# DeltaNet followed by soft-MoE slots: a planned instruction order, an inverse built from halves, and outputs re-laid on chip

## The chip, the cores and the metric

The kernel runs on one core of a Trainium2 chip. The metric is the device time of one execution in microseconds (us). Everything is fp32. The core has five instruction queues that run side by side and each take their instructions strictly in order: TensorE (PE, matrix products into PSUM), VectorE (DVE), ScalarE (ACT), GpSimd (POOL), and SyncE (SP), which here only issues DMAs. An instruction that waits holds up everything behind it on its own queue.

## The reference

Two blocks follow each other. The first is a delta-rule attention over 768 time steps for 4 batches and 8 heads of width 48; its output is laid out as 3072 tokens of 384 numbers. The second is a soft mixture of 8 experts with 4 slots each.

```python
k_n = k / (norm(k) + 1e-6)
for t in range(S):                              # S = 768, per batch and head, D = 48
    y[t] = q[t] @ state
    state += beta[t] * outer(k_n[t], v[t] - k_n[t] @ state)
x = y as (3072 tokens, 384)
logits = x @ phi                                # phi: 384 x 32 slots
d = softmax(logits, over tokens);  slot_in = d.T @ x          # 32 x 384
slot_out[e] = relu(slot_in[e] @ w1[e]) @ w2[e]  # w1: 384 x 1024, w2: 1024 x 384, 8 experts
out = softmax(logits, over slots) @ slot_out    # 3072 x 384
```

## The kernel before

**The scan.** Time is cut into 24 chunks of 32 steps; four chunks make a group, of which there are six. The 32 heads of all batches are handled together: the 128 partitions are four heads of a half-set times 32 steps, and the free dimension runs over 4 batches and 2 half-sets. Within a chunk the recurrence becomes matrix products. With T the inverse of a unit lower triangular 32x32 matrix made of beta and K K', a chunk computes the residual R = V - K S (`psR`, L278, then DVE at L283), solves U = T R (`psW`, L289, copied by ACT at L292), updates the state S += K' U (`psS`, L299, copied by ACT at L311 and DVE at L309 into the other of two block-diagonal state tiles), and gives Y = Q S + A U (`psY`, L278 and L316, copied at L318). Only R, U and S depend on the chunk before; everything else is preparation.

**Preparation** of a chunk (`prep`): K and Q arrive by DMA as 32-partition pieces (four DMAs of 48 KB for each tensor and chunk, L80), are padded from 48 to 64 columns, transposed on PE (L173) and copied by ACT (L176). Then Gram products of K with K and Q (L188) give the triangular matrix `Lc` and the masked `AT` (L195).

**Inversion** of a group (`invert`): DVE transposes `Lc` so that each partition holds one whole 32x32 matrix (128 matrices at once), the norms of k are formed by DVE and an ACT square root (L221 to L233), POOL scales the matrix (L230), and then 31 elimination steps run on DVE. Step j multiplies one row by one column into `pr` (L240) and subtracts that from all rows below (L243), so there are 62 operations, each of which needs the one before. POOL scales the result (L247), DVE transposes it back (L253).

**Routing** of a group (`route`): the outputs are transposed on PE with 96 columns at a time (L336), multiplied by phi (L345), and go through both softmaxes; the token softmax keeps a running maximum. `repeat` spreads the weights with products against the identity (L398), `slots` adds the weighted outputs in 64 small products (L410).

**Order.** A loop over chunks issues all of this. `chunk` calls `fill()` between its products; each call issues a quarter of a list in which the preparation of the chunk eight ahead, a quarter of the next group's inversion and a quarter of the last group's routing are interleaved evenly. Weights of two experts are loaded during the scan; all others get buffers only when the scan's pools are closed (`att.close()`). They arrive as whole 1.5 MB DMAs on SP.

**The tail**: two passes of four experts each (`first`: L543, relu, transposes L556; `second`: L567), a fold over experts, then 24 output tiles of 128 tokens (L593), copied by DVE and ACT in turn and stored through six buffers `ob` on SP.

## Time and profile before

| what | us |
|---|---|
| median of 3 runs (lowest, highest) | 493.28 (489.14, 493.31) |
| span of the profiled execution | 489.7 |
| elimination on DVE, L240 and L243, 186 instructions each, busy | 68.0 and 66.3 |
| residual L283, 24 instructions, mean of one | 0.55 |
| state copies, ACT L311 and DVE L309, mean of one | 0.80 and 0.96 |
| POOL products L230 and L247, six each, mean of one | 1.91 and 1.91 |
| weight loads w1 and w2, 8 each of 1.5 MB, median to landing | 8.2 and 15.1 |
| loads of K, Q, V, 96 of each, 48 KB, median to landing | 2.3 |

One execution was recorded by the hardware profiler. "Busy" is the time in which an engine had at least one instruction running. PEld is the loading of the stationary operand, which runs beside PE. The granted clock (PEclk) is a share of TensorE's full clock. A group is all instructions of one source line. An idle stretch of an engine is put down to whatever released it last. The chain is the work that ended last, followed backwards.

### The profile page before, as it was taken

How to read it: one execution, taken by the hardware profiler on the slowest of the kernel's cores; microseconds unless marked ns; L12 is line 12 of the kernel's file. 1: busy time of each engine (PE TensorE's matmuls, PEld its weight loads, DVE VectorE, ACT ScalarE, POOL GpSimd, SP SyncE). 2: the span in 40 equal slices, each digit the busy share in tenths (PEclk: the TensorE clock that was granted, in tenths of full speed). 3: DMA queues.
4: the chain of work that ended last, by engine and by line, in shares of the span. 5: the costliest groups of instructions: out<-in, count | busy, mean ns of one | idle time of the engine just before them, and what ended most of it. 6: DMA issues, size and time to landing. Idle time of an engine off the chain costs nothing.

```text
span 489.7 us, 20564 instructions
## 1 busy us (share of the span) xinstructions
PE 334.7 (68%) x9387; PEld 248.3 (51%) x9387; DVE 245.1 (50%) x679; ACT 128.9 (26%) x257; POOL 63.6 (13%) x88
## 2 busy tenths in 40 slices
PE   5743374656766758788677776876875865788586
PEld 4532263545645646666466655665664753532133
DVE  4159716972168942379721788325997212210033
ACT  2331122121322422332422233224312222111012
POOL 9210112012020040020210200202301000000000
PEclk9655556665766759755778577599798797799695
DMA  6557742320322213202221110010300029949427
GB/s 114 86 94 195 205 83 51 52 37 18 52 51 39 46 19 52 50 16 40 51 39 33 19 19 13 9 20 5 113 23 1 4 94 367 424 156 434 208 101 287
DMA packets 84759, 45.53 MB, mean 93 GB/s; under 512 B 79392, under 2 KB 82624, under 8 KB 82624
## 3 DMA queue, kind: packets, MB, share of 16 engines
q1 hardware_dynamic: 81920, 43.67, 32.4%
q8 instruction: 74, 1.21, 1.0%
q10 hardware_dynamic: 2176, 0.39, 0.4%
q0 software_dynamic: 576, 0.15, 0.3%
q14 instruction: 13, 0.11, 0.1%
HBM read 39.47 MB, written 4.72 MB: 90 GB/s over the span
## 4 chain that ended last, share of the span: by engine, by line
DVE 27%; issue 25%; PE 19%; SPq 10%; DMA 10%; POOL 5%; ACT 3%; DVEq 0%; POOLq 0%; ACTq 0%
DVE pr L240 9%; SPq L80 9%; DVE tt L243 9%; DMA w2t<-in_moe_w_dram 4%; PE pso L567 3%; DVE S L309 3%; PE psR L278 2%; PE pt L410 2%; DMA w1t<-in_moe_w_dram 2%; PE psY L278 2%; POOL lb L230 2%; DMA Q<-in_q_dram 2%; DVE TT L253 2%; PE ph L543 1%; DMA out_dram<-ob 1%
## 5 line engine op out<-in xcount | busy, mean ns | idle before, releaser
L240 DVE TENSOR_TENSOR pr<-tt,lb 128x31 f32<-128x31 f32 (+15 forms) x186 | 68.0, 365 | 17.7 <-POOL lb L230 12.2
L243 DVE TENSOR_TENSOR tt<-tt,pr 128x31 f32<-128x31 f32 (+15 forms) x186 | 66.3, 357 | 5.7
L289 PE MATMUL psW<-R,TT 32*32 32x48 f32 x1536 | 29.9, 242 | 47.0 <-DVE R L283 45.5
L173 PE MATMUL pt<-ident,K 128*128 128x128 f32 x96 | 36.0, 396 | 24.1 <-DVE AT L195 18.7
L289 PEld LDWEIGHTS psW<-R,TT 32*32 32x32 f32 x1536 | 25.7, 134 | 52.4 <-DVE R L283 49.3
L176 ACT ACTIVATE KQ<-pt 128x512 f32<-128x512 f32 x48 | 27.1, 595 | 73.9 <-PE pt L173 73.5
L278 PE MATMUL psR<-S,KQ 128*32 128x96 f32 x768 | 33.1, 324 | 17.7 <-DVE S L309 17.0
L316 PE MATMUL psY<-U,AT 32*32 32x48 f32 x1536 | 39.0, 256 | 3.2 <-issue 3.1
L195 DVE TENSOR_TENSOR AT<-pt,tri 128x128 f32<-128x128 f32 x48 | 11.9, 288 | 54.6 <-ACT Lc L194 54.4
L188 PE MATMUL pt<-KQ 48*32 48x64 f32 x1536 | 33.5, 246 | 6.2 <-ACT KQ L176 2.6
L309 DVE COPY S<-psS 48x768 f32<-48x768 f32 x23 | 22.1, 961 | 31.1 <-ACT S L311 30.7
L316 PEld LDWEIGHTS psY<-U,AT 32*32 32x32 f32 x1536 | 31.1, 143 | 9.2 <-issue 7.1
L299 PE MATMUL psS<-U,K 32*48 32x48 f32 x1472 | 25.3, 261 | 14.5 <-ACT U L292 11.6
L278 PEld LDWEIGHTS psR<-S,KQ 128*32 128x32 f32 x768 | 23.7, 145 | 22.4 <-DVE S L309 18.9
L188 PEld LDWEIGHTS pt<-KQ 48*32 48x32 f32 x1536 | 25.0, 119 | 16.0 <-ACT KQ L176 9.5
L173 PEld LDWEIGHTS pt<-ident,K 128*128 128x128 f32 x96 | 17.3, 186 | 30.7 <-DVE AT L195 20.2
L278 PE MATMUL psY<-S,KQ 128*32 128x96 f32 x768 | 32.3, 314 | 0.0
L292 ACT ACTIVATE U<-psW 128x384 f32<-128x384 f32 x24 | 11.8, 490 | 75.6 <-PE psW L289 75.6
L299 PEld LDWEIGHTS psS<-U,K 32*48 32x48 f32 x1472 | 20.4, 155 | 20.7 <-ACT U L292 15.7
L410 PE MATMUL pt<-Y,dr 32*32 32x97 f32 x768 | 25.1, 271 | 8.5 <-DVE AT L195 4.3
L230 POOL TENSOR_TENSOR lb<-lb,gm 128x1024 f32<-128x1024 f32 x6 | 11.5, 1911 | 141.0 <-DVE gm L229 141.0
L173 PE MATMUL pt<-ident,Q 128*128 128x128 f32 x96 | 29.7, 364 | 0.0
(124 smaller groups left out, 454.9 us busy)
## 6 DMA issues: line engine op xcount, KB each, us to landing
w1t<-in_moe_w_dram SPq DMA_DIRECT2D x8, 1536.0 KB, 8.2
w2t<-in_moe_w_dram SPq DMA_DIRECT2D x8, 1536.0 KB, 15.1
K<-in_k_dram SPq DMA_DIRECT2D x96, 48.0 KB, 2.3
V<-in_v_dram SPq DMA_DIRECT2D x96, 48.0 KB, 2.3
out_dram<-ob SPq DMA_DIRECT2D x24, 192.0 KB, 2.3
Q<-in_q_dram SPq DMA_DIRECT2D x88, 48.0 KB, 2.3
Q<-in_q_dram ACTq DMA_DIRECT2D x8, 48.0 KB, 3.0
bb<-in_beta_dram POOLq DMA_DIRECT2D x16, 6.0 KB, 3.0
```

Of the source, the lines that this page charges most:

```text
L80: eng.dma_start(out=dst[C * h:C * h + C, :, 0:D], in_=src.rearrange("b (g h) s d -> h s (b g) d", h=4)[h, cc * C:(cc + 1) * C])
L173: nc.tensor.transpose(tp[:, i, a, :], src[:, b * G:(b + 1) * G, :].rearrange("p g d -> p (g d)"), ident)
L176: nc.scalar.activation(KQ[cc][:, 2 * bh:2 * bh + 2], tp, ACT.Copy)
L188: nc.tensor.matmul(pg[g][rh, b], lhsT=KQ[cc][r, b, 0, rh], rhs=KQ[cc][r, b, :, rh], start=True, stop=True, skip_group_check=True)
L240: nc.vector.tensor_tensor(prv, tt[:, j, 0:m].unsqueeze(1).broadcast_to([P, w, m]), lb[:, j, j + 1:C].unsqueeze(2).broadcast_to([P, w, m]), ...
L243: nc.vector.tensor_tensor(tt[:, j + 1:C, 0:m], tt[:, j + 1:C, 0:m], prv, op=ALU.subtract)
L278: nc.tensor.matmul(dst[hs[h], b].rearrange("p g d -> p (g d)"), lhsT=kq[:, b, a, hs[h]], rhs=old[:, h, b, :], start=(b == 0), stop=False, ...
L289: nc.tensor.matmul(pw[hs[h], u], lhsT=T[hs[h], u], rhs=R[hs[h], u], start=(u == 0), stop=True, skip_group_check=True)
L299: nc.tensor.matmul(psS[DP * g:DP * g + D, h, b * D:(b + 1) * D], lhsT=K[hs[h], b * G + g, 0:D], rhs=Ut[hs[h], b * G + g], start=(cc == 0 a ...
L309: nc.vector.tensor_copy(dst, src)
L316: nc.tensor.matmul(py[hs[h], b, g], lhsT=at[hs[h], g, b], rhs=Ut[hs[h], b * G + g], start=False, stop=True, skip_group_check=True)
L410: nc.tensor.matmul(pa[r], lhsT=st["dr"][r, c, b, :], rhs=Yn[r, c, b, 0:GD + 1], start=(b == 0), stop=(b == B - 1), skip_group_check=True)
```

## The change

It is a rewrite of the whole kernel that computes the same thing.

*Order.* The kernel text no longer issues instructions; it records operations with the values they read and write, an engine (or a choice of two) and an assumed cost. `Plan.run` then places them: it repeatedly takes, for each engine, the operation of highest priority among those that can start within 0.15 us of the earliest one, and assigns buffers and PSUM banks as it goes. The priority is the longest path to the end by the assumed costs. The result is one fixed order for each queue. Evictions from PSUM, re-lay DMAs and stores get their engine from the plan.

*Memory.* All scan buffers lie in one arena, cut into pieces of the size of one expert weight (12 KB per partition). A first planning run tells in which order buffers die; they are packed into pieces in that order, and each piece becomes a weight buffer when all its members are dead. Weights are loaded in thirds (w1) and quarters (w2).

*Inverse.* The two diagonal 16x16 halves of the triangular matrix are inverted side by side in one set of 15 steps, 30 DVE operations; the lower left block is made on PE from two products of small tiles. The norms use two powers on POOL.

*Scan.* The state is no longer block-diagonal: reads of it become 32 products with 48 rows instead of 16 with 128. Half of the state accumulates in PSUM and is copied by ACT, the other half is added by DVE. K and Q lose their padding; their transposes are products with the identity as moving operand, 48 columns each.

*Routing.* Four DMAs per chunk move the output from its scan layout into rows of 32 tokens by 384, on chip. Transposes, logits and slot sums then run on whole 128-row tiles. beta arrives in one DMA and is spread by four products.

```diff
+    def run(self, backing=()):
...
+                t0 = min(c[0] for c in cands)
+                t, o, cost = max((c for c in cands if c[0] <= t0 + self.window),
+                                 key=lambda c: (c[1].prio, -c[0]))
...
-        def eliminate(j):
-            m, w = j + 1, C - 1 - j
...
+        for j in range(HC - 1):                                  # HC = 16
+            m, w = j + 1, HC - 1 - j
...
+                    nc.vector.tensor_tensor(
+                        o.rearrange("p (b i k) -> p b i k", b=2, i=w),
+                        t[:, j, :, 0:m].unsqueeze(2).broadcast_to([P, 2, w, m]),
+                        s[:, :, j + 1:HC, j].unsqueeze(3).broadcast_to([P, 2, w, m]),
+                        op=ALU.mult)
...
+                nc.vector.tensor_tensor(d, d, o, op=ALU.subtract)
...
+                            PE.matmul(t[hs[h], u], lhsT=sb(lc, C, C)[hs[h], u],
+                                      rhs=sb(M1, C, HC)[hs[h], u],
+                                      start=True, stop=True, skip_group_check=True)
...
+                            PE.matmul(t[hs[h], u], lhsT=sb(D0, C, C)[hs[h], u],
+                                      rhs=sb(P1, C, HC)[hs[h], u],
+                                      start=True, stop=True, skip_group_check=True)
...
+            PO.tensor_tensor(nrall[:, n], nrall[:, n], expo[:, 0:1].broadcast_to([P, C]),
+                             op=ALU.pow)
...
-                    nc.tensor.transpose(
-                        tp[:, i, a, :],
-                        src[:, b * G:(b + 1) * G, :].rearrange("p g d -> p (g d)"), ident)
+                        PE.matmul(t[rs_[g], b, :], lhsT=m[:, b, g, :], rhs=ident, start=True,
+                                  stop=True, skip_group_check=True)
...
-                    nc.tensor.matmul(dst[hs[h], b].rearrange("p g d -> p (g d)"),
-                                     lhsT=kq[:, b, a, hs[h]], rhs=old[:, h, b, :],
-                                     start=(b == 0), stop=False, skip_group_check=True)
+                            PE.matmul(t[hs[h], g, b * D:(b + 1) * D], lhsT=m[rs_[g], b, a, hs[h]],
+                                      rhs=s[rs_[g], h, b], start=(b == 0), stop=False,
+                                      skip_group_check=True)
...
+                copy(e, sb(new, 4, BD)[:, 0:2], banks[:, 0:2, 0:BD])
...
+                    nc.vector.tensor_tensor(sb(new, 4, BD)[:, 2:4], sb(old, 4, BD)[:, 2:4],
+                                            ps(ks)[:, :, 0:BD], op=ALU.add)
...
+                dge[e].dma_start(out=sb(X, B, G, 4, D)[hs[c], :, :, h], in_=sb(Yv, B, G, D)[hs[h]])
...
+    with tc.manual_schedule():
+        for o in sorted(plan.ops, key=lambda o: (o.start, o.prio)):
+            o.fn(o.eng)
```

In the code after, L503 are the new transposes, L473 the Gram products, L653 and L666 the coupling of the halves, L704 the reads of the state, L727 the solve, L748 the update, L771 the product with A, L715 the residual, L783 the re-lay DMAs, L799, L811 and L867 the routing's transposes, logits and slot sums, L922 and L930 the weight loads.

## The prediction

> **What bounds the kernel now.** I read the page's header and 40-slice picture first, then busy time by stage, then waits inside the scan, then single bursts.

> ```profile
> span 489.7 us, 20564 instructions
> PE 334.7 (68%) x9387; PEld 248.3 (51%) x9387; DVE 245.1 (50%) x679; ACT 128.9 (26%) x257; POOL 63.6 (13%) x88
> ...
> DVE  4159716972168942379721788325997212210033
> ...
> PEclk9655556665766759755778577599798797799695
> ```

> No engine is full on average; DVE swings between 1 and 9 six times, once per group of four chunks, and the TensorE clock sits near 0.7. By stage (us; PE, PEld, DVE, ACT, POOL busy, then clock, DMA share, GB/s):

> ```profile
> 0.00:63.00 63.00, 27.87 (x568) 21.39 (x568) 35.13 (x110) 14.97 (x31) 19.64 (x41) 0.63 0.66 138
> 63.00:399.00 336.00, 241.67 (x8092) 194.19 (x8096) 193.15 (x525) 99.30 (x193) 43.14 (x44) 0.73 0.18 34
> 399.00:424.00 25.00, 16.16 (x432) 12.85 (x420) 4.52 (x19) 4.83 (x11) 0.84 (x4) 0.73 0.91 357
> 424.00:471.00 47.00, 36.20 (x259) 12.72 (x259) 5.14 (x13) 4.10 (x10) 0.00 (x0) 0.89 0.60 247
> 471.00:489.70 18.70, 12.75 (x49) 7.14 (x48) 7.12 (x13) 5.67 (x12) 0.00 (x0) 0.67 0.71 254
> ```

> The scan takes 336 of 489.7 us: the residual R is formed first at 62.9 and last at 399.0, so 14.6 us per chunk over 23 intervals. PE is busy 72% of it, at 0.73 clock. The waits of that stretch name what PE stands for:

> ```profile
> PEld psW L289 <- DVE R L283: 49.1, 16, 10.4
> PE psW L289 <- DVE R L283: 45.5, 15, 10.1
> ```

> R is a 0.55 us instruction, but it is queued on DVE behind up to 10 us of elimination (L240 and L243, 134 us in all). Where no elimination runs, a chunk takes 8.1 us:

> ```profile
> 382.80 0.55 DVE L283 TENSOR_TENSOR R<-V,psR 128x384 f32<-128x384 f32 x1 [1.55 <-PE psR L278]
> ...
> 390.91 0.55 DVE L283 TENSOR_TENSOR R<-V,psR 128x384 f32<-128x384 f32 x1 [3.20 <-PE psR L278]
> ```

> So the scan is bound by DVE's queue and, beneath it, by PE. In the tail the chain holds a 17.8 us wait for expert weights (443.4 to 461.3): they start only when the scan's buffers are given up. The first chunk waits 63 us for loads, eight chunks of preparation and one whole inversion.

> [...] 32 passes of L345 took 2.40 us at clock 0.51 (409 to 412) and 26 took 0.79 us of loads at 1.00 (338): 75 against 30 ns. [...] The new 48-wide transposes are plain products, so I price them as full fp32 ones; the trace has no such tile. [...]

> **Part by part.** In the trace one fp32 product shows as two passes (L188: 32 products, 64 records), a transpose as one.

> *Elimination.* 62 dependent DVE operations per group become 30. Starts in the trace are spaced 0.255 us at 60 elements and 0.455 at 247: about 0.195 + 0.00105 n. Before: 62 x 0.195 + 10,912 x 0.00105 = 23.5 us; after: 30 x 0.195 + 2,720 x 0.00105 = 8.7 us. Six groups: 89 us of DVE less. Around it DVE loses eight norm operations (about 1.7 us), keeps a 1.23 us transpose, swaps the 1.92 us one for two of half size (2 us), gains one 512-element scaling and one subtraction (0.7 each). POOL loses two 1.91 us products. It gains two powers on 32 elements: not in the trace; 0.15 us (its smallest memset) to 1.9 us (its 1,024-element product) each, I take 0.4. They stand before the scaling at which DVE waits with the next R behind it, so the high end costs 6 x 3 = 18 us. ACT loses eight table loads of 1.28 us.

> *PE work per chunk*, at full clock, from weight-load bursts in 326 to 342:
> - transposes: 16 products, 32 passes; L345's 30 ns with four column tiles, doubled for two: 1.9 us (before 8 x 0.11 = 0.9). If packed as well as four, 1.0; never below zero gain, the work is added.
> - Gram products 64 passes: 1.0, unchanged.
> - reads R and Y: 32 products each instead of 16, half as wide: 64 passes at L188's 15 to 16 ns, 1.0 each (before 0.67).
> - L289, L299, L316 equivalents: 0.75, 0.71, 0.8, unchanged.
> - coupling of halves, new: 64 products, 128 passes at L289's 11.7 ns, 1.5.
> - routing per group: 12 transposes 1.3, logits 24 passes 0.7, slots 8 passes at L567's 87 ns 0.7, three transposes 0.3; 3.0/4 = 0.76 (before turns 2.6, logits 1.0, repeat 0.8, slots 2.6, rest 0.5: 1.9).

> After: 9.4 us; before by the same prices: 7.4. **PE work rises by a quarter.** Before really spent 10.5 us (241.7/23) at clock 0.73, 1.42 times its full-clock sum. After, DVE needs about 7.3 us per chunk by the same rows (elimination and its neighbours 3.4, R, mask and state 1.5, its share of evictions 1.9, routing 0.5), ACT about 4.5 with its 91 DMA issues, SP 361 issues x 0.485 = 175 us: PE alone is the bound. [...] I take clock 0.9, a factor 1.15 on the line from 1.0 to 1.42.

> *Recurrence.* Read 1.0, R 0.55, solve 0.75, copy 0.49, update 0.71, state 0.56, six handoffs of about 0.2: 5.3 us. The state copy was 0.80 then 0.96, one behind the other; now two halves on ACT and DVE side by side. What is late next is PE's other work.

> *Head.* The built program issues all eight chunks' preparation ahead of the first solve: 8 x 2.9 us plus 4 x 0.7 for split Gram products, from about 5.4 us (eight PSUM memsets go first): 32 us. The other path: 16 K loads on two queues land near 10.5, Lc at 13, then 1.2 + 2 + 0.7 + 8.7 + 2 + 2.3 + handoffs: 33. I take 36, against 62.9.

> *Scan.* Sixteen chunks still carry a preparation: 9.4 x 1.15 = 10.8 each, 173 us. Eight don't: (9.4 - 2.9) x 1.15 less what little inversion is left, 7.2 each, 58. Together 231, against 341 (62.9 to the last output copy, 404.1).

> *Tail.* All W1 issues now stand before the last re-lay DMA on SP, all 32 W2 issues behind it. Before, 22 MB came in 61.6 us (357 GB/s), so 12.6 MB take 35 us and land 36 us after the last output copy; from there before took 28.4 us (461.3 to 489.7): 64. By PE: re-lay DMAs (2 issues, about 2.5 us landing), transposes, logits and slots about 12 us instead of 23.2, expert products 31 plus turns 3, then 20.2 from 469.5 on: 66. I take 66, against 85.6. Out stores stay 18 us. The re-lay DMAs of earlier groups (96 x 48 KB, the loads' size) lie beside a DMA share of 0.18; without that cover each costs a load's 2.3 us.

> Sum: 36 + 231 + 66 = **333 us** against a span of 489.7. That run lies 0.7% under the median of 493.28, so I predict **335**.

> **Rivals.**
> - *Quick:* clock near 1.0 and well-packed transposes: 16 x 8.5 + 8 x 6.4 = 187, plus 34 and 62: 283; with transposes at 1.9, about 297. For: 320 to 340 ran at 1.00 with PE 82% busy. Against: 180 to 200 was 0.76 at 91%.
> - *Slow PE:* [...] At 0.73, factor 1.42: 16 x 13.3 + 8 x 8.5 = 281, plus 40 and 66: 387. Throughout at half clock: transposes 4.8, Gram 1.2, reads 2.2, others 3.5, coupling 2.6, routing 1.5: 15.8; 16 x 15.8 + 8 x 9.8 + 46 + 70 = 447.
> - *Slower than before:* the half clock plus an order whose waits come true late. Engines take their queues in order; where a planned cost is too low (powers on POOL, the scaling behind them), DVE stands there and R behind it, PE idles[...]. From 447 it takes 43 us more, 1.8 us of PE standing in each chunk. For: before shows just such 10 us stalls. Against: they came from 23.5 us of elimination, now 8.7.
> - *Weights not early:* if W1 also lands after the scan, 25 MB at 357 GB/s take 70 us and the tail is 98: 365.

> **How the numbers follow.** About 1% (5 us) is what a measurement can tell from no change. Likeliest case (300 to 365 us) 0.55; quick 0.17; slow PE or late weights above 365 but faster than before 0.23; within 1% 0.01; slower 0.04. Range 288 to 395 leaves some 0.06 below and 0.13 above. Faster 0.95.

> **What would show it.** Elimination 50 to 55 us on DVE; first solve near 36 us; residuals 10 to 11 us apart for sixteen chunks, then 7; PE over 85% busy in the scan at clock 0.85 or more; transposes (L503) about 46 us or more; tail 66 us with W2 landing last. I am wrong if PE stands waiting for DVE or POOL for more than 10% of the scan, if the clock stays under 0.75, or if the 48-wide transposes cost half my price.

## The result, and the profile after

The changed kernel is slower: 512.73 us (median, 509.47 to 516.88) beside 492.14 us (489.14 to 493.31) for the kernel before on the same chip, a ratio of 1.050 (95%: 1.040 to 1.060). The profiled execution spans 507.8 us against 489.7. The page's first parts, for the kernel after:

```profile
span 507.8 us, 29272 instructions
PE 344.6 (68%) x13716; PEld 274.9 (54%) x13716; DVE 181.4 (36%) x465; ACT 79.4 (16%) x162; POOL 128.1 (25%) x119
...
DVE  5436225502242512344333453334341122442232
...
PEclk9987559565586955597755885555675555767995
...
q8 instruction: 108, 1.77, 1.5%
...
PE 50%; issue 32%; DMA 6%; DVE 4%; POOL 3%; SPq 3%; ACT 1%; ACTq 1%; POOLq 0%; DVEq 0%
```

VectorE has lost 64 us of work and its six full swings, as foretold, and has all but left the chain of waits (4%). In its place stands "issue", 32% of the span: time in which the engine waited for nothing that the profile shows. Of these 160 us, 111 stand ahead of TensorE, in 93 pieces; 39 more are one stretch of GpSimd's queue in the tail (450 to 490). The kernel before had an entry of the same name:

```profile
q8 instruction: 74, 1.21, 1.0%
...
DVE 27%; issue 25%; PE 19%; SPq 10%; DMA 10%; POOL 5%; ACT 3%; DVEq 0%; POOLq 0%; ACTq 0%
...
63.65 15.09 issue
78.78 1.92 POOL lb L230
...
114.98 25.95 issue
140.97 1.92 POOL lb L230
```

It was another thing there: four stretches of 15 to 29 us on GpSimd's queue, two of them shown, make up 96 of its 124 us, and 10 us stand ahead of TensorE.

The chain of waits of the kernel after, in order of time (start, length, what), shows where TensorE's part lies:

```profile
110.54 0.81 PE banks L771 x64
111.35 0.05 PE banks L653 x5
111.40 1.95 issue
113.35 1.83 PE banks L653 x62
115.18 0.31 PE banks L704 x6
115.49 1.47 issue
116.96 0.97 PE banks L704 x55
117.93 1.08 PE banks L653 x70
119.01 1.68 issue
```

TensorE works off some 125 matmuls, stands for about 1 to 2 us in the middle of a group of independent products, and goes on. Counted in the trace, with weight loads and the few waits of its queue, these stops lie 256 instructions apart (the records numbered 2497, 2753, 3009, 3265, 3521 and so on): of TensorE's 92 stops over 0.6 us, 73 stand at this one place of a block of 256. At each a packet of 16,384 bytes has just come in on q8, the queue that the page names "instruction". TensorE's 13,716 matmuls, as many weight loads and 163 other records of its queue are 107.8 times 256, beside 108 packets; in the kernel before, twice 9,387 and 121 are 73.8 times 256, beside 74. So q8 is read here as TensorE's program, at 64 bytes an instruction. An fp32 product is four of them in the trace (two weight loads, two matmuls), so 64 products use up one packet. A stop ends about 1.4 us after the packet's landing, 2.5 us after the fetch began (medians).

Where the time went, from the same records (TensorE busy: at least one matmul or weight load under way; a gap counts as a fetch's if it is the longest that is open when a packet of q8 lands or begins within 0.6 us of it):

| us | before | after | difference |
|---|---|---|---|
| TensorE busy | 336.0 | 346.5 | +10.5 |
| idle at a fetch | 60.4 | 122.1 | +61.7 |
| idle otherwise | 93.0 | 38.8 | -54.2 |
| packets on q8 | 74 | 108 | +34 |

The three add up to the 18 us by which the span grew. The rule also takes in waits for other engines in which a packet happens to land, and these are most of the kernel before's 60 us: of its stops over 0.6 us, 9 (11 us) stand at the block's place, against 73 (112 us) in the kernel after. What ended TensorE's idle stretches says the same: waits for VectorE fell from 102 to 21 us and those for ScalarE from 22 to 3, while those for nothing that the profile shows rose from 12 to 116. So the gain was made, by these two counts some 100 us of waiting for others, and it was given back: 34 packets more, and fetches no longer hidden behind those waits.

### The profile page after: what moved, and what is told of

It reads as the page before. It is cut to its first block, busy times and chain, and to the rows that moved or that the text cites. A ratio compares the mean times of both kernels' runs of the same rounds, so it can differ in the third digit from the quotient of the medians.

```text
span 507.8 us, 29272 instructions
## 1 busy us (share of the span) xinstructions
PE 344.6 (68%) x13716; PEld 274.9 (54%) x13716; DVE 181.4 (36%) x465; ACT 79.4 (16%) x162; POOL 128.1 (25%) x119
## 4 chain that ended last, share of the span: by engine, by line
PE 50%; issue 32%; DMA 6%; DVE 4%; POOL 3%; SPq 3%; ACT 1%; ACTq 1%; POOLq 0%; DVEq 0%
PE banks L704 8%; PE banks L503 7%; PE banks L771 7%; PE banks L727 6%; PE banks L666 5%; PE banks L748 5%; PE banks L653 5%; PE banks L473 4%; SPq L439 3%; DMA arena<-in_q_dram 2%; PE banks L799 2%; DMA arena<-in_k_dram 1%; DMA arena<-arena 1%; PE banks L867 1%; POOL nrall L541 1%
## 5 line engine op out<-in xcount | busy, mean ns | idle before, releaser
L325 ACT ACTIVATE arena<-banks 128x384 f32<-128x384 f32 (+3 forms) x109 | 55.0, 507 | 372.2 <-PE banks L748 121.4
L327 DVE COPY arena<-banks 128x512 f32<-128x512 f32 (+3 forms) x77 | 43.2, 561 | 133.1 <-PE banks L503 38.5
L503 PE MATMUL banks<-ident,arena 128*48 128x128 f32 x768 | 63.7, 325 | 14.2 <-DMA arena<-in_k_dram 6.1
L704 PE MATMUL banks<-arena 48*32 48x48 f32 x2944 | 48.3, 254 | 30.0 <-issue 29.2
L503 PEld LDWEIGHTS banks<-ident,arena 128*48 128x48 f32 x768 | 53.3, 149 | 20.8 <-issue 13.4
L704 PEld LDWEIGHTS banks<-arena 48*32 48x32 f32 x2944 | 37.9, 130 | 40.7 <-issue 35.3
L771 PE MATMUL banks<-arena 32*32 32x48 f32 x1536 | 35.5, 256 | 16.2 <-issue 16.2
L727 PE MATMUL banks<-arena 32*32 32x48 f32 x1536 | 33.3, 246 | 18.0 <-issue 11.7
L473 PE MATMUL banks<-arena 48*32 48x64 f32 (+1 forms) x1792 | 29.5, 249 | 17.1 <-issue 8.9
L771 PEld LDWEIGHTS banks<-arena 32*32 32x32 f32 x1536 | 29.5, 145 | 20.7 <-issue 19.0
L727 PEld LDWEIGHTS banks<-arena 32*32 32x32 f32 x1536 | 28.1, 138 | 22.5 <-issue 14.5
L653 PE MATMUL banks<-arena 32*32 32x16 f32 x1536 | 24.8, 206 | 19.3 <-issue 18.7
L748 PE MATMUL banks<-arena 32*48 32x48 f32 x1472 | 26.4, 266 | 14.1 <-issue 14.1
L666 PE MATMUL banks<-arena 32*32 32x16 f32 x1536 | 26.3, 210 | 13.7 <-issue 13.5
L473 PEld LDWEIGHTS banks<-arena 48*32 48x32 f32 x1792 | 22.8, 122 | 22.5 <-issue 19.9
L653 PEld LDWEIGHTS banks<-arena 32*32 32x32 f32 x1536 | 22.4, 144 | 22.2 <-issue 20.2
L541 POOL TENSOR_TENSOR nrall<-nrall,expo 128x32 f32<-128x32 f32 x6 | 32.7, 5446 | 0.5
L666 PEld LDWEIGHTS banks<-arena 32*32 32x32 f32 x1536 | 24.0, 150 | 16.0 <-issue 15.7
L748 PEld LDWEIGHTS banks<-arena 32*48 32x48 f32 x1472 | 21.4, 160 | 20.0 <-issue 19.0
```

Source lines behind the costliest of these rows:

```text
L325: AC.activation(dst, src, ACT.Copy)
L327: nc.vector.tensor_copy(dst, src)
L473: PE.matmul(t[hs[h], g, b * n0:(b + 1) * n0], lhsT=kt[rs_[g], b, 0, hs[h]], rhs=rhs, start=True, stop=True, skip_group_check=True)
L503: PE.matmul(t[rs_[g], b, :], lhsT=m[:, b, g, :], rhs=ident, start=True, stop=True, skip_group_check=True)
L541: PO.tensor_tensor(nrall[:, n], nrall[:, n], expo[:, 0:1].broadcast_to([P, C]), op=ALU.pow)
L653: PE.matmul(t[hs[h], u], lhsT=sb(lc, C, C)[hs[h], u], rhs=sb(M1, C, HC)[hs[h], u], start=True, stop=True, skip_group_check=True)
```

## The experiments

**Theory 1:** TensorE's instructions come at 256 in about 3.6 us, and the change has moved the kernel from a bound by VectorE to this one. **Rivals:** A, TensorE's columns and clock set the pace; B, VectorE's elimination still does; C, the powers on GpSimd (5.45 us each) hold the inverses; D, small DMA packets crowd out the fetches; E, the order was planned with wrong prices. Ratios are to the kernel before on the same chip; "packets" are those on q8. In e4, e7 and e18 the order of instructions stays as it was; every other edited kernel is ordered anew by the planner, and its difference can hold a part of that.

| run | edit | us | ratio (95%) | packets |
|---|---|---|---|---|
| after | | 512.7 | 1.050 (1.040-1.060) | 108 |
| e7 | reads cut in two | 601.7 | 1.230 (1.222-1.238) | 131 |
| e18 | before, reads cut in two | 498.9 | 1.026 (1.021-1.031) | 86 |
| e15 | coupling left out | 440.6 | 0.905 (0.898-0.912) | 83 |
| e1 | whole-column inverse | 496.7 | 1.021 (1.014-1.029) | 83 |
| e2 | square roots for powers | 512.9 | 1.057 (1.047-1.066) | 107 |
| e3 | e1 and e2 | 496.3 | 1.014 (1.010-1.019) | 83 |
| e4 | 1536-byte loads | 497.4 | 1.025 (1.017-1.033) | 107 |
| e6 | block-diagonal reads | 521.0 | 1.064 (1.058-1.070) | 96 |
| e12 | e2 and block-diagonal reads | 486.8 | 0.995 (0.991-0.998) | 96 |
| e14 | e2 and one-pass transposes | 500.2 | 1.031 (1.024-1.039) | 103 |
| e10 | order by other prices | 520.4 | 1.069 (1.058-1.081) | 107 |
| e8 | e2, e6, e14 together | 479.1 | 0.978 (0.973-0.983) | 91 |
| e11 | e8 by other prices | 474.7 | 0.979 (0.971-0.988) | 91 |
| e16 | e11, wide state update | 460.9 | 0.948 (0.941-0.955) | 86 |
| e17 | e16, whole-column inverse | 417.5 | 0.855 (0.847-0.864) | 62 |

**The supply by itself.** TensorE runs through products that wait for nobody:

```
for i in range(n):        # 32x32 products of 48 columns, or of 1
    PE.matmul(banks[hs[i % 4], i // 4 % 4, 0:cols], lhsT=ident[hs[i % 4], 0:C],
              rhs=wide[hs[i % 4], 0:cols], start=True, stop=True, ...)
```

> TensorE alone on operands that are filled once, without the reference's computation (the output is zeros): 768 products of 32x32 by 48 columns while 150 loads in 192-byte packets run, then 160 products of 128x128 by 512 columns, 512 of 32x32 by 48 with the queues quiet, 256 of 128x128 by 128, 512 of 32x32 by 1, 768 transposes of 128x128, 192 products of 128x128 by 256 columns. No product waits for another engine. Theory 1: in the sections of small products TensorE stops at every 256th of its instructions for 1.2 to 2 us though nothing is waited for, under the loads 0.1 to 0.5 us longer than without; the products of 512 columns, whose queued work outlasts a fetch of about 2.4 us, show no stop. Rival A: no stops over 0.3 us in any section with the queues quiet. Rival D: stops under the loads alone.

Its chain of waits, in the section of 48 columns with the queues quiet (L68) and in that of one column (L72):

```profile
186.49 1.56 PE banks L68 x128
188.05 1.90 issue
189.94 2.03 PE banks L68 x128
191.97 1.70 issue
193.67 2.78 PE banks L68 x128
196.45 0.67 issue
197.13 2.78 PE banks L68 x128
199.91 0.95 issue
...
```

```profile
276.91 1.57 issue
278.48 1.88 PE banks L72 x128
280.36 1.85 issue
282.21 1.88 PE banks L72 x128
284.09 1.85 issue
```

128 matmuls and their 128 weight loads, a stop, and again. What the reader is to see is the sum: 1.56 + 1.90, 2.78 + 0.67, 1.88 + 1.85: always 3.4 to 3.8 us. Whether the products had 48 columns or one, and at which clock they ran, made next to no difference here: fetches began every 3.66 us on average (48 columns), 3.59 (one column) and, beside running loads of 192-byte packets, 3.85. The sections of 128, 256 and 512 columns have no stop over 0.3 us: there 256 instructions are 14 us of work and more. A window of each kind (busy TensorE, weight loads, VectorE, GpSimd; then clock, DMA share, GB/s):

```profile
186.50:193.60 7.10, 3.58 (x256) 3.25 (x256) 0.00 (x0) 0.00 (x0) 0.81 0.02 5
197.20:208.00 10.80, 8.27 (x384) 7.70 (x384) 0.00 (x0) 0.00 (x0) 0.50 0.02 5
...
213.00:269.00 56.00, 56.00 (x606) 55.88 (x607) 0.00 (x0) 0.00 (x0) 1.00 0.00 1
```

The same stream went at clock 0.81 and at 0.50, at one pace. Under the loads, where Theory 1 allowed the stops 0.1 to 0.5 us more, a block took some 0.2 us more. So Rivals A and D fall for such streams, since the stops are there with one column and without traffic, and a low clock is here no cause of lost time.

**Instructions added, work unchanged.** Each product of the two state reads is cut in two, in the kernel after and in the one before:

```
-  PE.matmul(t[.., b*D:(b+1)*D], lhsT=m[..], rhs=s[rs_[g], h, b], ..)
+  for i in range(2):
+      f = slice(i * D // 2, (i + 1) * D // 2)
+      PE.matmul(t[.., b*D:(b+1)*D][:, f], lhsT=m[..], rhs=s[rs_[g], h, b, f], ..)
```

> The changed kernel with every product of the two state reads (L704) cut into two of 24 columns: the same columns and results, 1472 products and 5888 TensorE instructions more, 23 blocks of 256. No wait, eviction or other engine's instruction changes. Theory 1 (supply of 3.6 us per block at best): 23 x 3.6 to 4.1 = 83 to 94 us more: 590 to 602 us, 131 instruction packets on q8. Rival A (columns and clock): 508 to 520 us.

> The kernel before with each product of its two state reads (L278) cut into two of 48 columns: the same columns and results, 768 products, 3072 TensorE instructions, 12 blocks of 256 more (86 packets in place of 74). At the changed kernel's price for such a cut (92 us for 23 blocks, 4.0 each) it would be 48 us slower, 535 us. Theory 1: the kernel before takes about 5.0 us per block in its scan, since it waits for VectorE's elimination, and only 21 of 64 blocks come at the supply's own 3.5 to 4 us, so that about a third to a half of the added supply shows: 503 to 515 us. If instructions cost it nothing: within 5 us of 488.

The kernel after takes 88 us more for 23 packets (1.230 less 1.050, of 490), 3.8 us each: the whole price. No other engine was touched, and PE and issue are the entries of the chain that grew (in the trace TensorE's busy time by 55 us, its idle time at fetches by 42; that a product's own time isn't what sets the pace is shown by the stream, not by this run):

```profile
q8 instruction: 131, 2.15, 1.5%
...
PE 51%; issue 34%; DMA 5%; DVE 4%; POOL 3%; SPq 2%; ACT 0%; ACTq 0%; POOLq 0%; DVEq 0%
```

The kernel before takes 13 us more for 12 packets, about 1 us each, less than the theory foretold: most of the supply was hidden behind its waits. In its scan fetches began 5.05 us apart in the median, and 3.73 us apart in the scan after: 60 of 87 intervals there are under 4 us, 21 of 64 before.

**Instructions taken away.**

```
-  PE.matmul(t[hs[h], u], lhsT=sb(lc, C, C)[hs[h], u], rhs=sb(M1, C, HC)[hs[h], u], ..)
-  copy(e, sb(P1, C, HC)[:, s], ps(p1, C, HC)[:, s])
-  PE.matmul(t[hs[h], u], lhsT=sb(D0, C, C)[hs[h], u], rhs=sb(P1, C, HC)[hs[h], u], ..)
-  nc.vector.tensor_tensor(sb(T, C, C)[:, s, HC:C], sb(M1, C, HC)[:, s], ps(p2, C, HC)[:, s], ..)
+  nc.vector.tensor_tensor(sb(T, C, C)[:, s, HC:C], sb(M1, C, HC)[:, s], sb(D0, C, C)[:, s, 0:HC], ..)
```

> The changed kernel with the coupling's products (L653, L666) and the eviction between them left out: the off-diagonal block of each inverse is put together from the two halves without the Gram block between them, so the result is not the reference's; every other instruction stays, VectorE's elimination by halves with it. 1536 products, 6144 TensorE instructions, 24 blocks of 256 fewer. Theory 1 at the full supply rate: 24 x 3.6 to 4.1 = 86 to 98 us less, 410 to 425 us; at the 2.3 us a block that block-diagonal reads gave back, 453 us. If the coupling's removal is worth no more than with the whole-column inverse (11 us), so that another wait of the scan takes over at once: 490 us or more.

> The changed kernel with the inverse again over all 32 columns on VectorE, so without the coupling products on TensorE (L653, L666) and their masks; everything else as in the changed kernel. It issues 1536 products fewer, at four TensorE instructions each 24 blocks of 256 instructions fewer. Theory 1 (TensorE stops about 1.5 us at most blocks of 256 of its instructions, while 16 KB of them are fetched, and this is what took the expected gain): 24 x 1.47 = 35 us of stops and up to 51 us of coupling work go, the longer elimination costs about 15 us ahead of the first solve: 420 to 455 us, 84 instruction packets on q8 in place of 108, VectorE busy about 90 us longer without setting the pace. Rival A (TensorE's work alone sets the pace, the stops do not follow the instruction count): the coupling's 51 us less 15 us: about 470 us. Rival B (VectorE's elimination sets the pace): slower than the changed kernel, 540 us or more.

> The whole-column inverse on VectorE without coupling products, as in the first run of these (497 us), with the two powers of 5.45 us replaced by ScalarE's square root and VectorE's steps. In that run TensorE had 83 blocks and the chain of waits put 16% on GpSimd and 20% on VectorE. If, once the coupling is off TensorE, the latency of an inverse sets the pace, six times 10.9 us = 65 us of powers come off the chain: 430 to 450 us. If TensorE's supply alone still sets it, the powers are worth the head's 11 us at most: 485 to 497 us.

That is e15; e1 takes out the whole block of halves, masks and coupling, and eliminates 32 columns as the kernel before did. Without the coupling's products, and VectorE's elimination as it was, the kernel loses 71 us (0.145 of 490) for 25 packets, 2.8 us each; their busy time was 51 us. That is less than the 86 to 98 us of the full supply rate: GpSimd, with the powers, now holds 16% of the chain. An eviction and its wait went too, so that the 71 us aren't shown to be the supply's alone. The whole-column inverse takes the same packets away and gains 14 us only, far from Theory 1's 420 to 455 us and in none of its rivals' ranges. Its scan is shorter by much more: from the first solve to the last chunk's, 334 us in place of 387. But the first solve comes 29 us later, and VectorE is back in the chain:

```profile
PE 37%; DVE 20%; POOL 16%; issue 14%; DMA 10%; ACT 1%; SPq 1%; ACTq 0%; DVEq 0%; POOLq 0%
...
L613 PE MATMUL banks<-arena 48*32 48x48 f32 x2944 | 47.5, 252 | 64.5 <-DVE arena L672 34.0
```

The 34 us are one wait, at the second chunk: the state's eviction (L672) stands in VectorE's queue behind 21 us of elimination and then two powers for which VectorE waits. In all, TensorE waits 88 us for VectorE in e1, against 21 in the kernel after, and still 59 for nothing shown, against 116. So Rival B holds in part for the whole-column inverse and is wrong for the halves. That the powers are off the path as well (e3) shortens that one wait to 22 us, but the whole gained nothing that can be told, against the larger of its two forecasts.

**Fewer, wider products.** The state is kept block-diagonal, so that one product of 96 columns reads two heads; or K and Q are padded to 64 columns, and four transposes do the work of eight products:

```
-  for g in range(G):
-      PE.matmul(t[hs[h], g, ..], lhsT=m[rs_[g], b, a, hs[h]], rhs=s[rs_[g], h, b], ..)
+  PE.matmul(t[hs[h], b // 2, b % 2, 0:G * D], lhsT=m[:, b, a, hs[h]], rhs=s[:, h, b], ..)
...
-  PE.matmul(t[rs_[g], b, :], lhsT=m[:, b, g, :], rhs=ident, ..)
+  PE.transpose(t[:, b], m[:, b], ident)
```

> The changed kernel with the two state reads (L704) as 16 products of 96 columns in place of 32 of 48: the state is kept block-diagonal over the pair of heads, and its evictions are split over the two partition halves (about 0.5 us more per chunk on the recurrence). The columns that TensorE streams stay the same; 736 products fall away, 2944 TensorE instructions, 11.5 blocks of 256. Theory 1, sharpened by the stream run (TensorE is supplied with 256 instructions in about 3.6 us at best, whatever the products' size): 11.5 blocks x 3.6 to 4.1 us = 41 to 47 us less, up to 12 us given back by the evictions: 460 to 480 us beside the changed kernel's 508. Rival A (TensorE's own work and its clock set the pace, counted in columns): no gain, 505 to 520 us.

> Block-diagonal reads once more, now on the changed kernel with square roots in place of the powers (513 us), and with one buffer of KQ and of AT given up for the larger state in place of one of V and of Q. In the first such run (521 us) a late V buffer held GpSimd's queue, with the powers behind it, for some 20 us at one chunk, and the first solve came 11 us later. Theory 1: 11.5 blocks fewer, 41 to 47 us, less up to 12 us for the split evictions: 465 to 485 us. If the reads of 96 columns[...] and the evictions cost what the fewer instructions save: 505 to 520 us.

> The changed kernel with square roots in place of the powers (513 us) and with K and Q padded to 64 columns, so that 8 one-pass transposes take the place of 16 two-pass products in every chunk; one buffer each of Q, KQ and AT given up for the padding. 1152 TensorE instructions fewer, 4.5 blocks. Theory 1 with the supply alone: 16 to 18 us less, 495 us. Rival A, the work alone: the transposes' busy time falls from 64 to 36 us as in the run with all three edits, 28 us less, 485 us. Both: about 470 us.

The first, e6, missed: 521 us, 12 packets fewer and yet no gain. Its chain of waits points to what the edit brought along, one buffer of V given up for the larger state:

```profile
223.92 2.25 DMA arena<-arena
226.19 0.31 SPq L446
226.54 2.26 DMA arena<-in_v_dram
229.05 0.83 POOL arena L698
...
230.25 5.46 POOL nrall L548
...
236.19 5.45 POOL gmall L551
...
243.88 0.46 DVE arena L772
```

A V load stands behind a re-lay transfer on SP, the scaling of V (L698) waits for it on GpSimd, and the powers, VectorE and the next state read wait behind that: 20 us at one chunk, and the first solve came 11 us later. With other buffers given up and square roots for the powers (e12), the same reads gain 30 us against e2, 2.5 us a packet, just short of the forecast (487 us, 465 to 485 foretold); which of the two changes freed the gain wasn't separated. The transposes (e14 against e2) gain 12 us for 5 packets, 2.5 each, less than the 16 to 18 of the supply alone and than the 22 us by which their busy time fell (65.3 to 43.7).

**Powers, packets, order.**

```
-  PO.tensor_tensor(nrall[:, n], nrall[:, n], expo[:, 0:1].broadcast_to([P, C]), op=ALU.pow)
+  AC.activation(nrall[:, n], ssall[:, n], ACT.Sqrt)                                (e2)
...
-  in_=src.rearrange("b (g h) s d -> h s (b g) d", h=4)[h, cc * C:(cc + 1) * C]
+  in_=src.rearrange("b g s d -> (b g s d)").rearrange("(r x) -> r x", x=U * D)[     (e4)
+      (4 * cc + h) * C:(4 * cc + h + 1) * C]
...
-  op(f"W{cc}", [("PE", 0.7)], ..)
+  op(f"W{cc}", [("PE", 1.8)], ..)          and all small products likewise         (e10)
```

> The changed kernel with the two powers on GpSimd (5.45 us each) replaced by the kernel before's way, a square root on ScalarE and short steps on VectorE. Theory 1 (instruction fetch on TensorE): only the head gets shorter, by the two powers that stand on the path to the first solve, 10.9 us: 495 to 505 us, with the number of stops on TensorE unchanged at about 76 over 0.3 us. Rival C (the powers hold the inverses and through them the scan): six groups of 10.9 us, 65 us: about 445 us.

> The changed kernel with the K, Q and V loads reading rows of 1536 bytes that lie together, in place of eight pieces of 192 bytes: the same bytes in an eighth of the packets; the rows are others than the reference's, so what is computed is not its result. Theory 1: the fetch of instructions goes from 1.09 us to about 0.9 us, 108 x 0.15 = 16 us, and the waits for loads ahead of 100 us (part of the 6% of the chain put down to DMA, 30 us) go in part: 465 to 500 us, and the stops remain at most boundaries of 256 instructions. Rival D (the stops come from the crowding of the DMA engines by small packets): the stops fall under 0.5 us each: about 400 us.

> The changed kernel's own instructions in another order: the planner is told 1.8 us for each group of 32 small products (32 x 4 instructions x 14 ns, the rate of the stream run) in place of 0.5 to 0.7, 1.0 us for 8 transposing products, 12 us for the powers in place of 2, and the routing's bias is 150 in place of 30, without which it finds no order. Theory 1 (supply of TensorE's instructions): their number is the same, so 490 to 515 us. Rival E (the loss comes from an order planned with prices that are too low, so that waits fall where the plan has none): 430 to 460 us.

None of the three moves the kernel as its rival has it. Square roots change nothing that can be told (1.057 and 1.050, intervals overlap): even the head's 11 us, which Theory 1 granted, did not show, and the first solve starts at 51.5 us as against 51.9. The longer rows give 12 us, but idle time at fetches is 124 us, as in the kernel after (122), so the gain isn't there. The other order is no faster (520 us): its first solve comes 15 us later, and its scan, to the last output product, is 8 us shorter, 384 in place of 392, which is far from what 430 to 460 us in all would need. Rivals C, D and E fall for the kernel after; with the coupling gone, the powers stand in the chain again (e1, e15).

**Towards a faster kernel.**

```
-  for g in range(G): PE.matmul(dst[rs_[g], b*D:..], lhsT=m[hs[h], b*G + g], rhs=r[hs[h], b*G + g], ..)
+  PE.matmul(dst[:, b*G*D:(b + 1)*G*D], lhsT=m[hs[h], b], rhs=r[hs[h], b], ..)      (e16, e17)
```

> The changed kernel, inverse by halves kept, with three edits: block-diagonal state reads, K and Q padded to 64 columns so that 8 one-pass transposes of 128x128 take the place of 16 products (each of two passes), and the powers replaced by square root and short steps. TensorE loses 4096 instructions, 16 blocks of 256. Theory 1: 16 x 3.6 to 4.1 = 58 to 66 us less, the head's 11 us less, up to 12 us given back by the evictions: 440 to 460 us, under the kernel before. Rival A: the transposes' work alone falls, 64 to about 22 us of busy time at the measured rate of 113 ns a pass, and the head's 11: about 455 to 465 us at most if all of that lies on the path.

> The run of the changed kernel with block-diagonal reads, one-pass transposes and square roots (479 us), ordered with the prices of the run before this one (1.2 us for the 16 wider reads, 0.5 for 4 transposes; routing's bias 80). Its 91 blocks of TensorE instructions at 3.6 us leave 328 us, so that the order has something to win: Theory 1 with a part for the order: 450 to 475 us. Rival E: below 440 us. If the order matters in neither: 475 to 485 us.

> The 475 us kernel (inverse by halves; block-diagonal reads, one-pass transposes, square roots, the planner's corrected prices) with the state update as 16 products over pairs of heads, 128 rows by 96 columns of which the off-diagonal blocks are not used, in place of 32 of 48 by 48: 736 products, 2944 TensorE instructions, 11.5 blocks fewer (80 left of the 91). Theory 1 at 2.3 to 3.6 us a block: 26 to 41 us less, 434 to 449 us. If the wider products' own work and the waits between engines set the pace by now: 465 to 480 us.

> The same edits as in the run before, with the whole-column inverse in place of halves and coupling: about 55 blocks of TensorE instructions, 200 us of supply, VectorE about 85 us busier. If supply still counts: 420 to 440 us. If VectorE's elimination and the chunks' chain of waits set the pace, as the two runs with the whole-column inverse suggest (497 and 496 us): 465 to 490 us.

e16's expectation counted the products wrongly: 368 fall away, not 736, and 5 packets; it gained 15 us, 3 each. e8 gained less than foretold, and the order added nothing sure to it (0.979 and 0.978). The whole-column inverse, worth 14 us as long as the rest of the chunk was made of small products, is worth 45 us on top of e16 (0.948 to 0.855), 1.9 us for each of 24 packets, and this kernel, 14.5% faster than the one before, has another bound:

```profile
span 415.3 us, 17764 instructions
PE 277.8 (67%) x7860; PEld 211.0 (51%) x7860; DVE 284.7 (69%) x724; ACT 89.2 (21%) x183; POOL 40.9 (10%) x70
...
q8 instruction: 62, 1.02, 1.0%
...
DVE 36%; PE 20%; DMA 18%; issue 13%; ACT 4%; SPq 3%; POOL 2%; ACTq 2%; POOLq 0%; DVEq 0%
```

VectorE leads again, with 62 packets' supply (62 x 3.6 = 223 us) well under the span. Why e3, with 83 packets and the same elimination, stayed at 496 us, its trace tells in part: TensorE waits 91 us for VectorE there and 62 for nothing shown, in e17 83 and 16. The elimination's part is about the same in both; what e17 has lost is the supply's part and 31 us of TensorE's busy time (309 and 278).

## Why the prediction was wrong

- *What bounds the kernel before*: half read. VectorE's queue did set the pace (TensorE waited 102 us for it and 12 for nothing shown), but "beneath it, PE" was read as TensorE's work alone, and the 1.42 between its time and its full-clock sum was put down to the clock.
- *Elimination*, 52 us foretold: L587, L603 and L582 come to 45.5 us. Right, and VectorE left the chain.
- *Powers*, 0.4 us taken within 0.15 to 1.9: each took 5.45 us on 32 elements a partition, outside both bounds. It cost nothing that could be told (e2).

```profile
L541 POOL TENSOR_TENSOR nrall<-nrall,expo 128x32 f32<-128x32 f32 x6 | 32.7, 5446 | 0.5
```

- *PE work per chunk*, the step that failed, and with it the scan (231 us foretold, 390 measured). It priced passes by their time in full bursts, 11.7 to 16 ns, with clock as the only thing that could stretch them (1.15 from 1.0 to 1.42); the 0.9 behind that factor was the author's estimate, which no trace showed. In the scan from 54 to 444 us TensorE was busy 265 us, against 231 foretold for the scan, at clock 0.63: that size is 15% off (the new transposes alone took 63.7, against 46; that price, twice the 30 ns of L345, was an estimate as well). What the sum has no term for is the other 125 us, most of it stops at fetches. As an estimate by the stream's rate, the supply makes a product cost 56 ns (3.6 us over 64), with 48 columns as with one: the coupling's 64 products a chunk 3.6 us, not 1.5; and a chunk, with four packets (95 over 24), 14.3 us, not 9.4 by work. The measured scan is 390 / 24 = 16.3 us a chunk. The instruction counts were known beforehand, and the rate stood in the trace of the kernel before, where a tenth of the intervals between fetches in the scan are 3.5 us or less and 9 stops stand at the block's place.
- *The slow case*, TensorE at a low clock (0.73): the clock was lower still, 0.674 over the span, and the text named a clock under 0.75 as a sign of being wrong. But the stream kept one pace at 0.50 and at 0.81: here a low clock went with the lost time, and as its cause it isn't shown. Nor did a run show what lowers the clock. (The 75 against 30 ns of L345 set matmuls beside weight loads: like with like, matmuls took 75 and 41 ns a pass there, loads 48 and 30.)
- *The rival that ended slower* had VectorE stand behind planned costs that are too low. VectorE and GpSimd hold 4% and 3% of the chain (the sign named was waits for them in over 10% of the scan), and the order with higher prices (e10) is no faster: right in its sign, wrong in its mechanism.
- *Head*, 36 us: the first solve ran at 52 to 54, with two powers, 11 us, in its chain; without them (e2) other work took their place and it came no sooner. The second chunk's solve followed 35 us later; from 67.8 to 82.1 us the chain there is a re-lay transfer and SP's queue with loads of K and Q. *Tail*, 66 us: from the last output product at 444.4 us, 63.4. The second weights came from 446 to 482, last as foretold; that part, with products of 128 to 512 columns, has no stop over 0.6 us at the block's place, with three packets, and its prices held. (The 22 MB in 61.6 us that it reckoned from were 20.6 in the trace, 334 GB/s, so that the 35 us for 12.6 MB came out right by some luck.)

## What to carry to other kernels

Count TensorE's instructions (four for an fp32 product, two for a transpose) and set 256 of them against 3.6 us before pricing columns: where products are as small as here and few waits are left to hide the fetches, this line bounded the stage, and there neither the planner's other prices nor, in the stream, the clock moved the pace. An edit that takes work off another engine by adding small products to TensorE pays for their supply, 1 us a packet in the kernel before, 3.8 in the kernel after. Merging products, even with columns that are thrown away, gained 2.5 to 3 us a packet here where no buffer was missed (e12, e14, e16). And an "issue" share in the chain of waits is to be asked on which engine it stands: in the kernel before it was GpSimd's queue, in the kernel after mostly TensorE's supply.
